# Pooling the next batch's keys on GpSimd: 256-column pieces, one per step, in place of a whole block every twelfth step

## The chip, the cores and the metric

The kernel runs on one core of a Trainium2 chip. The metric is the device time of one execution in microseconds; the time of a kernel is the median of its runs. The engines are named as in the profile: PE (TensorE) multiplies matrices, DVE (VectorE) and ACT (ScalarE) work elementwise, POOL (GpSimd) works elementwise too and issues indirect DMAs, SP (SyncE) issues the other DMAs.

## The reference

Attention with keys that are pooled 4 by 4 and projected, followed by a mixture of eight experts with one expert per row and a test that lets rows skip it:

```python
def _attn_ref(q, kv, w_sr):          # q (4, 12288, 128), kv (4, 384, 32, 128)
    kv_pool = kv.reshape(B, H // r, r, W // r, r, C).mean(axis=(2, 4))   # r = 4
    kv_flat = kv_pool.reshape(B, -1, C) @ w_sr                           # 768 keys a batch
    k = v = kv_flat
    s = scale * (q @ k.transpose(0, 2, 1))
    s = s - s.max(-1, keepdims=True)
    a = np.exp(s)
    a /= a.sum(-1, keepdims=True) + 1e-09
    return (a @ v).astype(np.float32)

def _moe_ref(x, w_skip, w_gate, w1, w2):   # x: the rows of the attention
    do_compute = x @ w_skip > 0
    out = x.copy()
    xc = x[do_compute]
    logits = xc @ w_gate
    e_idx = np.argmax(logits, axis=1)
    ...
    for e in range(E):
        mask = e_idx == e
        h = np.maximum(xc[mask] @ w1[e], 0.0)
        y[mask] = gate_w[mask, None] * (h @ w2[e])
    out[do_compute] = xc + y
    return out
```

## The kernel before

The program has two phases. The first is attention, one unrolled loop over 384 steps; a step is a tile of 128 query rows, and 96 steps are a batch. The second is a loop over groups of 2,048 rows for one expert each. The change lies in the first phase.

In step `t` the program records, in this order, `scores(t)` (six matmuls, L578 to L580), `attend(t - 6)` (18 matmuls with the probabilities as weights, L641), `p_transpose(t - 1)` (L616), the row maximum on DVE (L586), the exponential on ACT (L591), and for the tile before the split of the probabilities into two f16 halves: the high half on ACT (L595), the low half on DVE (L599, which reads `p_sb` and `p16`, both in SBUF). SP then transposes four of the six blocks by DMA (L603); the other two are transposed on PE and split by L623 (ACT) and L624 (DVE). DVE also inverts the row sums (L649, L651), which `attend` waits for through its accumulator's buffer.

Each engine runs its instructions in the order of recording and waits only where it needs another's result, so POOL can run ahead of the steps or fall behind them.

POOL's queue in the loop holds four kinds of work. Every fourth step it computes `q_lo` (L567), after ACT's `q_hi` (L566); the scores use it some six steps later. Every twelve steps a dozen finished tiles are routed to experts by `route`: POOL does part of it (L692 to L708, L721 `oh_all`, L756 `nxt` to L760), in turns with DVE, and PE counts rows with `oh_all` (L748, L749). It then issues twelve indirect DMAs, the scatters (L184), two per step. And it pools the keys of the next batch.

For that pooling SP loads a block of keys in four parts (`load_kv`, L413; the list `KV_T` of L897 sets the steps), at steps 9, 22, 35, 48, 61 and 74 of a batch the last part of blocks 0 to 5. Four steps after the last part the block's generator `pool_kv` joins the list `pools`. It halves the 2,048 columns of a partition by adds: 1,024, 512, 256 and a last add of 128 columns into `pooled`. The loop pops a generator only in steps with `tb % 12 == 11` (L964; `PSL` is 11) and runs it to its end there, so all four adds stand together. From step 84 on, `prep_kv` transposes and projects the pooled keys. Batch 0 has no step to hide in: most of its blocks are pooled on DVE (`pool_kv_first`), one by `pool_kv` in the prologue (L865). Batch 3 has no next batch, so nothing is pooled in its steps; pad rows are written there in place of the key loads.

Of the kernel before, what the change touches and what calls it, by code (L numbers as in the profile page):

```python
# [15 lines left out]
ALU = mybir.AluOpType  # L16
# [4 lines left out]
RT = 12  # L21
# [3 lines left out]
def kernel(  # L25
# [11 lines left out]
    nc = tc.nc  # L37
    NR, C, RT, P = q.shape
# [7 lines left out]
    E, _, FF = w1.shape  # L46
# [22 lines left out]
    PSL = 11  # L69
# [94 lines left out]
    def alloc_h(pool):  # L164
        h.update(hi=pool.tile([P, FC, ST], F16, name="h_hi"), lo=pool.tile([P, FC, ST], F16, name="h_lo"))

    op = ctx.enter_context(tc.tile_pool(name="op", bufs=2))
# [199 lines left out]
    with ExitStack() as p1:  # L367
# [32 lines left out]
        def write_pads(e, i):  # L400
            dst = scr[e * CAP + i * P:e * CAP + (i + PK) * P, :].rearrange("(p k) c -> p k c", p=P)
            no_dep(nc.sync.dma_start(dst, pad).ins, "scr")
# [5 lines left out]
        def load_kv(b, k, rs=range(R)):  # L408
            if rs[0] == 0:
                KVT[b, k] = kvp.tile([P, R, R * C], F32, name="kvt")  # L410
            src = kv[b, k * HG * R:(k + 1) * HG * R].rearrange("(i r) (g w) c -> r i g (w c)", r=R, w=R)
            for r in rs:
                nc.sync.dma_start(KVT[b, k][:, r, :], src[r])  # L413

        def pooled_out(b, k):
            if k == 0:
                pooled[b] = kprep.tile([P, KC, C], F32, name="pooled")
            return KVT.pop((b, k)), pooled[b][:, k, :]
# [12 lines left out]
        def pool_kv(b, k):  # L431
            t, o = pooled_out(b, k)
            f = t.rearrange("p r x -> p (r x)")
            n = R * R * C
            while n > 2 * C:
                n //= 2
                nc.gpsimd.tensor_tensor(out=f[:, 0:n], in0=f[:, 0:n], in1=f[:, n:2 * n], op=ALU.add)
                yield
            nc.gpsimd.tensor_tensor(out=o, in0=f[:, 0:C], in1=f[:, C:2 * C], op=ALU.add)

        HK = NK // 2
# [95 lines left out]
        def prep_kv(b):  # L537
            for f in (kv_transpose, k_matmul):
                for h in range(2):
                    f(b, h * HC, (h + 1) * HC)  # L540
                    yield
            yield from prep_v(b)
# [6 lines left out]
        def load_q(g):  # L549
            r, o = divmod(g, RG)  # L550
            q_sb[g] = qp.tile([P, GW], F32, name="q_sb")
            nc.sync.dma_start(q_sb[g], q[r][:, o * GT:(o + 1) * GT, :].rearrange("c t p -> c (t p)"))
# [5 lines left out]
        def run_late(q):  # L558
            while q:
                q.pop(0)()  # L560
# [9 lines left out]
        def scores(t):  # L570
            g, j = divmod(t, GT)
            k_hi, k_lo = KV[t // TPB][0:2]
            q_hi, q_lo = (x[:, j * P:(j + 1) * P] for x in qT[g])
            s = ps_s.tile([P, 2, 512], F32, name="s_ps")
            S_PS[t] = s
            for h in range(2):
                sl = slice(h * HK, (h + 1) * HK)
                nc.tensor.matmul(s[:, h, :HK], q_hi, k_hi[:, sl], start=True, stop=False)  # L578
                nc.tensor.matmul(s[:, h, :HK], q_hi, k_lo[:, sl], start=False, stop=False)  # L579
                nc.tensor.matmul(s[:, h, :HK], q_lo, k_hi[:, sl], start=False, stop=True)  # L580
# [3 lines left out]
        def row_max(t):  # L584
            NM[t] = small.tile([P, 1], F32, name="nm")
            nc.vector.tensor_reduce(out=NM[t], in_=S_PS[t][:, :, :HK], axis=AX.XY, op=ALU.max, negate=True)  # L586

        def row_exp(t):
            g, j = divmod(t, GT)
            P_SB[t] = pp.tile([P, 2, HK], F32, name="p_sb")  # L590
            nc.scalar.activation(out=P_SB[t], in_=S_PS.pop(t)[:, :, :HK], func=AF.Exp, bias=NM.pop(t))  # L591

        def p_hi(t):
            P16[t] = hl.tile([P, 2, KD * P], F16, name="p16")
            nc.scalar.activation(out=P16[t][:, 0, :], in_=p_flat(t)[:, 0:KD * P], func=AF.Copy, scale=2.0 ** PEXP)  # L595

        def p_lo(t):
            p16 = P16.pop(t)
            nc.vector.scalar_tensor_tensor(out=p16[:, 1, :], in0=p_flat(t)[:, 0:KD * P], scalar=2.0 ** PEXP,  # L599
                                           in1=p16[:, 0, :], op0=ALU.mult, op1=ALU.subtract)  # L600
            P_SB.pop(t)
            PT[t] = ptp.tile([P, 2 * KD, P], F16, name="pt")
            nc.sync.dma_start_transpose(PT[t], p16.rearrange("p a x -> p (a x)"))  # L603
# [6 lines left out]
        def p_transpose(t):  # L610
            g, j = divmod(t, PP)
            if j == 0:
                PTP[g] = acc_ps()
            p = p_flat(t)
            for i in range(KP):
                nc.tensor.transpose(PTP[g][:, (j * KP + i) * P:(j * KP + i + 1) * P],  # L616
                                    p[:, (KD + i) * P:(KD + i + 1) * P], ident)
            if j < PP - 1:
                return
            ps = PTP[g][:, 0:PP * KP * P]  # L620
            hl_t = ptq.tile([P, 2, PP * KP * P], F16, name="ptq")
            PTQ[g] = hl_t.rearrange("p a (j k x) -> p a j k x", j=PP, x=P)
            next_a.append(lambda: nc.scalar.activation(out=hl_t[:, 0, :], in_=ps, func=AF.Copy, scale=2.0 ** PEXP))  # L623
            next_v.append(lambda: nc.vector.scalar_tensor_tensor(  # L624
                out=hl_t[:, 1, :], in0=ps, scalar=2.0 ** PEXP, in1=hl_t[:, 0, :], op0=ALU.mult, op1=ALU.subtract))
# [268 lines left out]
        pools = []  # L894
# [14 lines left out]
        while t < NTILE + LAG - 1 or jobs:  # L909
            t += 1  # L910
            b, tb = divmod(t, TPB)
            live = t < NTILE
            for now, nxt in ((split_a, next_a), (split_v, next_v), (late_a, next_l)):
                now.extend(nxt)
                nxt.clear()
            if live:
                scores(t)
            if 0 <= t - LAG < NTILE:
                attend(t - LAG)
            if 0 <= t - 1 < NTILE:  # L920
                p_transpose(t - 1)
            if live:
                row_max(t)
            run_late(early_a)
            run_late(split_a)
            if 0 <= t - 1 < NTILE:
                p_hi(t - 1)
            run_late(late_a)
            if live:
                row_exp(t)  # L930
            run_late(early_g)
            run_late(split_v)
            run_late(early_v)
            if 0 <= t - 1 < NTILE:
                p_lo(t - 1)
            if live:
                if t % GT == 0 and t // GT + RG < NGRP:
                    load_q(t // GT + RG)
                if b + 1 < B:
                    for k, r in KV_T.get(tb, ()):  # L940
                        load_kv(b + 1, k, [r])
                if b + 1 < B and tb == PREP_T:
                    preps.append(prep_kv(b + 1))
                if t in PAD_T:
                    write_pads(*PADS.pop(0))
            first_step(NTILE - t)
            if t == NTILE:
                p_s.close()
                p_kv.close()
                alloc_h(p1.enter_context(tc.tile_pool(name="hp1", bufs=1)))  # L950
                ps_up = p1.enter_context(tc.tile_pool(name="ps_up", bufs=4, space=PSUM))
                alloc["h"] = lambda: ps_up.tile([P, ST], F32, name="up_ps")
            ph = t % GT
            if ph == 1 and t // GT + 2 < NGRP:
                q_split(t // GT + 2)
            ranked = run_jobs(ph)
            if preps and not ranked and (ph in (0, 3) or tb < LAG):
                if next(preps[0], "end") == "end":
                    preps.pop(0)
            if live and b + 1 < B:  # L960
                for k, r in KV_T.get(tb - 4, ()):
                    if r == R - 1:
                        pools.append(pool_kv(b + 1, k))
                if pools and tb % RT == PSL:  # L964
                    for _ in pools.pop(0):
                        pass
            for _ in range(2 * (t >= NTILE)):
                next(first)
        for _ in make_table():
# [76 lines left out]
```

## Time and profile before

| | us |
|---|---|
| median of 3 runs | 2067.53 |
| lowest, highest | 2058.41, 2076.75 |
| the profiled execution | 2057.81 |
| its span | 2056.1 |
| the attention loop's 384 steps, from the span's start | 35 to 1180 |
| mean granted TensorE clock | 0.949 |

The profiled execution is one run, 9.7 us under the median. Below, rows of the page and of the trace's views are shown as they stand. A row of instructions gives line, engine, operation, tiles, shapes and count, then busy time and mean duration in ns, then the engine's idle time just before them and what ended it. A row of waits gives who waited for what, the total in us, how often, and the longest. A row of a stage gives its limits and length, the busy time of each engine that is asked for with the count of instructions, and the granted clock, the DMA engines' busy share and GB/s. Batch 0 is steps 0 to 95, and so on; "dozen" stands for twelve steps from a multiple of twelve on.

### The profile page before, as it was taken

How to read it: one execution, taken by the hardware profiler on the slowest of the kernel's cores; microseconds unless marked ns; L12 is line 12 of the kernel's file. 1: busy time of each engine (PE TensorE's matmuls, PEld its weight loads, DVE VectorE, ACT ScalarE, POOL GpSimd, SP SyncE). 2: the span in 40 equal slices, each digit the busy share in tenths (PEclk: the TensorE clock that was granted, in tenths of full speed). 3: DMA queues.
4: the chain of work that ended last, by engine and by line, in shares of the span. 5: the costliest groups of instructions: out<-in, count | busy, mean ns of one | idle time of the engine just before them, and what ended most of it. 6: DMA issues, size and time to landing. Idle time of an engine off the chain costs nothing. (4 is left out here: it accounts for less than half of the span.)

```text
span 2056.1 us, 42524 instructions
## 1 busy us (share of the span) xinstructions
PE 1830.2 (89%) x13955; PEld 1308.1 (64%) x13955; DVE 1549.2 (75%) x3222; ACT 1302.8 (63%) x2480; POOL 1068.9 (52%) x1296
## 2 busy tenths in 40 slices
PE   4998888989898888898988867999999999999997
PEld 3987878878787787887878733444444444444443
DVE  7987857878686787776867746777777777777776
ACT  3876767767676676766767724656565655555564
POOL 2277674677756768655565753343333333333433
PEclk9999988999999899988999978999999999999999
DMA  7998988889789789878997832433333343333333
GB/s 173 209 193 173 184 165 165 182 157 167 147 161 170 156 177 184 169 164 175 191 185 169 176 73 74 107 98 88 92 88 92 88 103 100 94 90 90 91 89 88
DMA packets 620914, 284.61 MB, mean 138 GB/s; under 512 B 502112, under 2 KB 570848, under 8 KB 620768
## 3 DMA queue, kind: packets, MB, share of 16 engines
q1 hardware_dynamic: 599264, 244.30, 58.3%
q0 software_dynamic: 21504, 38.43, 6.2%
q8 instruction: 83, 1.36, 0.3%
q14 instruction: 63, 0.52, 0.1%
HBM read 90.60 MB, written 78.64 MB: 82 GB/s over the span
## 5 line engine op out<-in xcount | busy, mean ns | idle before, releaser
L184 POOL DMA_INDIRECT out_dram<-o,xin x288 | 299.7, 1040 | 510.7 <-DVE o L293 422.9
L586 DVE TENSOR_REDUCE nm<-s_ps 128x1 f32<-128x768 f32 x384 | 363.7, 947 | 208.7 <-PE s_ps L580 129.8
L270 DVE SCALAR_TENSOR_TENSOR h_lo<-h_ps,h_hi 128x512 f16<-128x512 f32 x544 | 343.1, 685 | 174.1 <-ACT h_hi L269 174.1
L591 ACT ACTIVATE p_sb<-s_ps,nm 128x768 f32<-128x768 f32 x384 | 346.5, 902 | 195.2 <-DVE nm L586 152.9
L184 POOL DMA_INDIRECT scr<-rows,di x384 | 385.5, 1004 | 149.6 <-issue 122.9
L641 PE MATMUL acc_ps<-v_hi,pt 128*128 128x138 f16 x3072 | 339.9, 232 | 90.8 <-DVE ptq L624 36.1
L641 PEld LDWEIGHTS <-pt 128*128 128x128 f16 x4608 | 294.2, 101 | 166.1 <-issue 164.9
L269 ACT ACTIVATE h_hi<-h_ps 128x512 f16<-128x512 f32 x544 | 298.9, 594 | 41.8 <-PE h_ps L268 17.9
L599 DVE SCALAR_TENSOR_TENSOR p<-p_sb,p 128x512 f16<-128x512 f32 x384 | 316.2, 824 | 1.6 <-ACT p L595 1.0
L578 PE MATMUL s_ps<-k_hi,q_hi 128*128 128x384 f32 x768 | 305.1, 397 | 7.6 <-issue 7.6
L641 PE MATMUL acc_ps<-v_lo,pt 128*128 128x138 f16 x1536 | 309.7, 231 | 2.2 <-issue 2.2
L579 PE MATMUL s_ps<-k_lo,q_hi 128*128 128x384 f32 x768 | 268.7, 350 | 4.9 <-issue 4.9
L580 PE MATMUL s_ps<-k_hi,q_lo 128*128 128x384 f32 x768 | 267.6, 348 | 5.7 <-issue 5.7
L595 ACT ACTIVATE p<-p_sb 128x512 f16<-128x512 f32 x384 | 242.0, 630 | 5.5 <-DMA pt<-p 2.2
L266 PE MATMUL h_ps<-xT,w_hi 128*128 128x512 f16 x544 | 206.1, 379 | 24.9 <-issue 24.9
L285 ACT ACTIVATE yT<-y_ps,y_sc 128x512 f32<-128x512 f32 x68 | 46.7, 687 | 276.9 <-PE y_ps L282 217.1
L282 PE MATMUL y_ps<-h_hi,w_hi 128*128 128x512 f16 x544 | 206.2, 379 | 0.0
L282 PE MATMUL y_ps<-h_hi,w_lo 128*128 128x512 f16 x544 | 206.2, 379 | 0.0
L268 PE MATMUL h_ps<-xT,w_lo 128*128 128x512 f16 x544 | 206.1, 379 | 0.0
L267 PE MATMUL h_ps<-xT,w_hi 128*128 128x512 f16 x544 | 206.1, 379 | 0.0
L282 PEld LDWEIGHTS <-w_hi 128*128 128x128 f16 x1152 | 113.4, 98 | 134.7 <-issue 4.5
L567 POOL TENSOR_TENSOR q_lo<-q_sb,q_hi 128x512 fp32r<-128x512 f32 x96 | 125.9, 1312 | 138.0 <-ACT q_hi L566 137.7
(215 smaller groups left out, 3283.7 us busy)
## 6 DMA issues: line engine op xcount, KB each, us to landing
kvt<-in_kv_dram SPq DMA_DIRECT2D x96, 256.0 KB
q_sb<-in_q_dram SPq DMA_DIRECT2D x96, 256.0 KB
out_dram<-rows SPq DMA_DIRECT2D x96, 256.0 KB
xin<-scr SPq DMA_DIRECT2D x75, 264.0 KB, 2.7
w_raw<-in_moe_w_dram SPq DMA_DIRECT2D x38, 512.0 KB, 4.0
scr<-pad SPq DMA_DIRECT2D x32, 264.0 KB
pt<-p SPq DMA_TRANSPOSE x384
scr<-rows,di POOLq DMA_INDIRECT x384
```

The costliest lines, as they stand in the source:

```text
L184: ins = nc.gpsimd.indirect_dma_start(out=dst, out_offset=bass.IndirectOffsetOnAxis(ap=ids, axis=0), in_=src, in_offset=None, bounds_check= ...
L269: nc.scalar.activation(out=h["hi"][:, c, :], in_=ps, func=AF.Relu)
L270: nc.vector.scalar_tensor_tensor(out=h["lo"][:, c, :], in0=ps, scalar=0.0, in1=h["hi"][:, c, :], op0=ALU.max, op1=ALU.subtract)
L282: nc.tensor.matmul(ps, w[:, c, :], h[x][:, c, :], start=(i == 0), stop=(i == len(terms) - 1))
L578: nc.tensor.matmul(s[:, h, :HK], q_hi, k_hi[:, sl], start=True, stop=False)
L579: nc.tensor.matmul(s[:, h, :HK], q_hi, k_lo[:, sl], start=False, stop=False)
L580: nc.tensor.matmul(s[:, h, :HK], q_lo, k_hi[:, sl], start=False, stop=True)
L586: nc.vector.tensor_reduce(out=NM[t], in_=S_PS[t][:, :, :HK], axis=AX.XY, op=ALU.max, negate=True)
L591: nc.scalar.activation(out=P_SB[t], in_=S_PS.pop(t)[:, :, :HK], func=AF.Exp, bias=NM.pop(t))
L595: nc.scalar.activation(out=P16[t][:, 0, :], in_=p_flat(t)[:, 0:KD * P], func=AF.Copy, scale=2.0 ** PEXP)
L599: nc.vector.scalar_tensor_tensor(out=p16[:, 1, :], in0=p_flat(t)[:, 0:KD * P], scalar=2.0 ** PEXP, in1=p16[:, 0, :], op0=ALU.mult, op1=ALU ...
L641: nc.tensor.matmul(ps[:, j % 2, :], w, v[a][:, k, :], start=(i == 0), stop=(i == len(AVL) - 1))
```

## The change

Each add of 1,024 or 512 columns is cut into adds of 256 columns, four and two of them, so that a block takes seven adds of 256 and the last one of 128. The generator yields after each of the seven. The loop no longer waits for the twelfth step: in every step it advances the first generator of the list once, from step 74 of a batch on twice. So block 0 is pooled in steps 13 to 20, block 1 in 26 to 33, block 2 in 39 to 46, block 3 in 52 to 59, block 4 in 65 to 72, and block 5 in 78 to 81. The sums are the same, in the same grouping. `pool_kv` in the prologue is cut in the same way.

```diff
@@ -432,10 +432,12 @@
             t, o = pooled_out(b, k)
             f = t.rearrange("p r x -> p (r x)")
             n = R * R * C
+            m = 2 * C
             while n > 2 * C:
                 n //= 2
-                nc.gpsimd.tensor_tensor(out=f[:, 0:n], in0=f[:, 0:n], in1=f[:, n:2 * n], op=ALU.add)
-                yield
+                for c in range(0, n, m):
+                    nc.gpsimd.tensor_tensor(out=f[:, c:c + m], in0=f[:, c:c + m], in1=f[:, n + c:n + c + m], op=ALU.add)
+                    yield
             nc.gpsimd.tensor_tensor(out=o, in0=f[:, 0:C], in1=f[:, C:2 * C], op=ALU.add)
 
@@ -961,9 +963,9 @@
                 for k, r in KV_T.get(tb - 4, ()):
                     if r == R - 1:
                         pools.append(pool_kv(b + 1, k))
-                if pools and tb % RT == PSL:
-                    for _ in pools.pop(0):
-                        pass
+                for _ in range(2 if tb >= 74 else 1):
+                    if pools and next(pools[0], "end") == "end":
+                        pools.pop(0)
```

The lines behind the first piece move by two in the kernel after (L437 becomes L439, L439 becomes L441, L567 becomes L569, and so on).

POOL's queue before, in the dozen of steps 24 to 35 of batch 0 (`scr<-rows,di` are the scatters, `oh_all` the table that PE's count waits for):

```order
L184 DMA scr<-rows,di 409600x132 x6
L567 TENSOR_TENSOR q_lo<-q_sb,q_hi 128x512
L184 DMA scr<-rows,di 409600x132 x2
L721 TENSOR_TENSOR oh_all_94<-oh,act 128x12x8
L184 DMA scr<-rows,di 409600x132 x2
L437 TENSOR_TENSOR kvt<-kvt 128x1024
L437 TENSOR_TENSOR kvt<-kvt 128x512
L437 TENSOR_TENSOR kvt<-kvt 128x256
L439 TENSOR_TENSOR pooled<-kvt 128x128
```

The same place after:

```order
L439 TENSOR_TENSOR kvt<-kvt 128x256
L184 DMA scr<-rows,di 409600x132 x2
L439 TENSOR_TENSOR kvt<-kvt 128x256
L184 DMA scr<-rows,di 409600x132 x2
L439 TENSOR_TENSOR kvt<-kvt 128x256
L184 DMA scr<-rows,di 409600x132 x2
L441 TENSOR_TENSOR pooled<-kvt 128x128
L569 TENSOR_TENSOR q_lo<-q_sb,q_hi 128x512
L184 DMA scr<-rows,di 409600x132 x2
L723 TENSOR_TENSOR oh_all_94<-oh,act 128x12x8
L184 DMA scr<-rows,di 409600x132 x2
```

The pooling has moved from behind the last scatters of the dozen to between the earlier ones, and ahead of `oh_all`.

POOL's queue before, in the last dozen of batch 0 but one, steps 78 to 83:

```order
L184 DMA scr<-rows,di 409600x132 x6
L567 TENSOR_TENSOR q_lo<-q_sb,q_hi 128x512
L184 DMA scr<-rows,di 409600x132 x2
L721 TENSOR_TENSOR oh_all_95<-oh,act 128x12x8
L184 DMA scr<-rows,di 409600x132 x2
L437 TENSOR_TENSOR kvt<-kvt 128x1024
L437 TENSOR_TENSOR kvt<-kvt 128x512
L437 TENSOR_TENSOR kvt<-kvt 128x256
L439 TENSOR_TENSOR pooled<-kvt 128x128
L449 MEMSET v_hi 128x6
```

The same place after, with two pieces in a step (the `v_hi` memset belongs to step 84):

```order
L439 TENSOR_TENSOR kvt<-kvt 128x256 x2
L184 DMA scr<-rows,di 409600x132 x2
L439 TENSOR_TENSOR kvt<-kvt 128x256 x2
L184 DMA scr<-rows,di 409600x132 x2
L439 TENSOR_TENSOR kvt<-kvt 128x256 x2
L184 DMA scr<-rows,di 409600x132 x2
L439 TENSOR_TENSOR kvt<-kvt 128x256
L441 TENSOR_TENSOR pooled<-kvt 128x128
L569 TENSOR_TENSOR q_lo<-q_sb,q_hi 128x512
L184 DMA scr<-rows,di 409600x132 x2
L723 TENSOR_TENSOR oh_all_95<-oh,act 128x12x8
L184 DMA scr<-rows,di 409600x132 x2
```

Here all eight adds come ahead of `q_lo` and `oh_all`. The queues of PE, DVE, ACT and SP hold the same work in the same order as before.

## The prediction

> **What bounds the kernel now.** The page comes first: which engine is busy where.
>
> ```profile
> PE 1830.2 (89%) x13955; PEld 1308.1 (64%) x13955; DVE 1549.2 (75%) x3222; ACT 1302.8 (63%) x2480; POOL 1068.9 (52%) x1296
> L586 DVE TENSOR_REDUCE nm<-s_ps 128x1 f32<-128x768 f32 x384 | 363.7, 947 | 208.7 <-PE s_ps L580 129.8
> L599 DVE SCALAR_TENSOR_TENSOR p<-p_sb,p 128x512 f16<-128x512 f32 x384 | 316.2, 824 | 1.6 <-ACT p L595 1.0
> ```
>
> The change touches only the attention loop, 384 steps (L586 runs once in each). An average hides that a dozen steps have two parts, so I asked for the stages of one dozen, all engines and then L586 alone, and for DVE's waits in each of them.
>
> ```profile
> 391.80:411.40 19.60, 19.60 (x220) 18.31 (x218) 19.08 (x39) 17.64 (x34) 10.83 (x19) 1.00 0.98 202
> 411.40:426.40 15.00, 10.88 (x93) 9.59 (x92) 7.27 (x15) 7.54 (x13) 12.88 (x13) 0.89 0.72 120
> 391.80:411.40 19.60, 8.46 (x9) 1.00 0.98 202
> 411.40:426.40 15.00, 2.87 (x3) 0.89 0.72 120
> DVE nm L586 <- PE s_ps L580: 0.3, 1, 0.3
> DVE nm L586 <- PE s_ps L580: 6.4, 2, 5.6
> ```
>
> (Rows 1 and 2: length, then PE, PEld, DVE, ACT, POOL busy, granted clock, DMA share, GB/s. Rows 5 and 6 belong to the first and the second stage.) Nine steps run smoothly in 19.60 us: PE is never idle, the DMA share is 0.98, and DVE is busy for 19.08 and waits for 0.3. The next three steps take 15.00 us: the clock falls to 0.89, DVE is half idle and waits for the scores. So in the smooth part DVE has 19.60 - 19.08 = 0.52 us to spare per dozen, and in the stalled part it has 7.73.
>
> The pooling of before runs at the seam. Here it is in the timeline of that dozen:
>
> ```profile
> 386.41 4.90 POOL L437 TENSOR_TENSOR kvt<-kvt 128x1024 f32<-128x1024 f32 x3
> 386.89 2.47 DVE L599 SCALAR_TENSOR_TENSOR p<-p_sb,p 128x512 f16<-128x512 f32 x1
> 390.98 0.28 PE L641 MATMUL acc_ps<-v_hi,pt 128*128 128x138 f16 x2 [0.18 <-DVE rs L649]
> 395.69 0.69 DVE L599 SCALAR_TENSOR_TENSOR p<-p_sb,p 128x512 f16<-128x512 f32 x1
> ```
>
> L599, which takes 0.69 us undisturbed, takes 2.47 when it meets a pooling add; PE loses 0.18 us by it here. The Trainium skill, "SBUF — State Buffer", section "Who interferes with whom", says that a VectorE instruction with two SBUF inputs (L599 is one) contends with a GpSimd instruction that reads SBUF, and that the second one to issue blocks until the first has finished. These rows agree.
>
> **The change part by part.** What the adds cost on POOL now, by shape:
>
> ```profile
> L437 POOL TENSOR_TENSOR kvt<-kvt 128x1024 f32<-128x1024 f32 x19 | 45.4, 2389 | 15.1 <-DMA kvt<-in_kv_dram 14.9
> L437 POOL TENSOR_TENSOR kvt<-kvt 128x512 f32<-128x512 f32 x19 | 28.9, 1519 | 1.5
> L437 POOL TENSOR_TENSOR kvt<-kvt 128x256 f32<-128x256 f32 x19 | 17.8, 936 | 1.5
> L439 POOL TENSOR_TENSOR pooled<-kvt 128x128 f32<-128x128 f32 x19 | 10.7, 561 | 1.5
> L437 POOL TENSOR_TENSOR kvt<-kvt x57: 722/1602/2419, 19.8 to 859.2; 128x1024 f32<-128x1024 f32 x19, 128x512 f32<-128x512 f32 x19, 128x256 f32<-128x256 f32 x19
> ```
>
> *POOL time.* A block was 2.39 + 1.52 + 0.94 + 0.56 = 5.4 us; it becomes seven pieces of 0.72 (the fastest seen) to 0.94 (the mean) and the last add, 5.6 to 7.1 us. Over 18 blocks in the loop that is 4 to 31 us more. POOL has room for it:
>
> ```profile
> POOL nxt L756 <- DVE pre L752: 127.4, 28, 6.8
> POOL q_lo L567 <- ACT q_hi L566: 109.2, 43, 9.2
> ```
>
> It idles 127.4 us before `nxt` and 109.2 before `q_lo` in the loop, so this costs nothing by itself.
>
> *What is taken away: the long blocks of L599.* Three stages of 72 steps each, the first two with five blocks pooled (L437 alone, 15 adds), the third with none; then L599 alone; then the two waits of PE that DVE ends, stage by stage:
>
> ```profile
> 349.80:561.10 211.30, 24.86 (x15) 0.93 0.86 165
> 636.70:852.40 215.70, 24.33 (x15) 0.94 0.88 175
> 932.00:1148.40 216.40, 0.00 (x0) 0.93 0.89 183
> 349.80:561.10 211.30, 60.15 (x72) 0.93 0.86 165
> 636.70:852.40 215.70, 64.09 (x72) 0.94 0.88 175
> 932.00:1148.40 216.40, 53.53 (x73) 0.93 0.89 183
> PE acc_ps L641 <- DVE ptq L624: 9.4, 4, 2.7
> PE acc_ps L641 <- DVE rs L649: 4.3, 6, 3.4
> PE acc_ps L641 <- DVE ptq L624: 9.7, 3, 4.1
> PE acc_ps L641 <- DVE rs L649: 8.9, 7, 3.7
> PE acc_ps L641 <- DVE ptq L624: 6.5, 4, 2.7
> PE acc_ps L641 <- DVE rs L649: 5.2, 3, 2.5
> ```
>
> On DVE: 72 undisturbed-by-pooling L599 cost 53.53 x 72/73 = 52.8, so pooling added 7.4 and 11.3 us, 18.7 over ten blocks, 1.87 a block, 33.6 us over 18. That is the gain if every blocked microsecond were on the path. On PE: its waits for DVE are 13.7 and 18.6 us with pooling, 11.7 without: 2.0 + 6.9 over ten blocks, 0.89 each, 16 us over 18. On the clock of the wall: 72 steps take 211.30 and 215.70 us with pooling and 216.40 without, so pooling costs nothing that can be seen (the third stage has the pad writes in place of the key loads, near enough the same DMA share). Bounds 0 and 33.6; I take 8, between the wall's 0 and PE's 16, since the block falls where PE is cold and DVE has been idle.
>
> *What is put in: 126 pieces, most of them in the smooth part,* where DVE has 0.52 us a dozen. How often does a short POOL add catch L599? From the stage without pooling: L599 takes 53.53/73 = 0.733 there against 0.69 undisturbed, 0.043 x 73 = 3.2 us, and this row of L567 alone gives the adds of `q_lo` that mostly did it:
>
> ```profile
> 932.00:1148.40 216.40, 23.34 (x18) 0.93 0.89 183
> ```
>
> 3.2/23.34 = 0.135 us of block per us of such an add. The pieces and last adds are 18 x 5.6 = 101 us of POOL, so 13.6 us; a piece is 0.72/1.30 as long, so the mean block is shorter: 7.5. From the other side, by L437 itself: 33.6 us of block for 18 x 5.4 = 97 us, 0.35 per us; the block grows with the add's length, and the length that a us of adding sits in falls from (2.39² + 1.52² + 0.94²)/4.85 = 1.84 to about 0.8, so 101 x 0.35 x 0.8/1.84 = 15 us. Of 7.5 to 15 us, the spare 0.52 x 18 = 9 takes some: 0 to 15 on the path; I take 6, nearer the `q_lo` row, which was measured in that very part.
>
> *Moves with one answer.* The pieces stand ahead of `oh_all` now, up to six of them, 6 x 0.72 = 4.3 us; the matmul that waits for it comes 10.7 us after it:
>
> ```profile
> 194.32 0.64 POOL L721 TENSOR_TENSOR oh_all<-oh,act 128x96 bf16<-128x96 f32 x1
> 205.69 0.21 PE L748 MATMUL misc<-oh_all,ones_bf 128*128 128x104 bf16 x1
> ```
>
> So 6 us remain, and it costs nothing; without the stall in between it would cost PE a few us in that dozen. The first piece asks for a load issued four steps before (some 9 us); of the DMAs whose landing the page gives, the nearest in size took
>
> ```profile
> xin<-scr SPq DMA_DIRECT2D x75, 264.0 KB, 2.7
> ```
>
> so POOL should seldom wait, and what would be queued behind it (`q_lo`, the scatters) is wanted later still. In the prologue one block also runs in pieces, 0.2 to 1.7 us later; PE waits there for POOL now, but afterwards for DVE for longer:
>
> ```profile
> 24.87 0.47 PE L454 MATMUL acc_ps<-ident,pooled 128*128 128x128 f32 x1 [1.61 <-POOL pooled L439]
> 31.58 0.47 PE L454 MATMUL acc_ps<-ident,pooled 128*128 128x128 f32 x1 [3.43 <-DVE pooled L428]
> ```
>
> 3.43 us of slack covers it. For prep at step 84 the pooled keys are ready earlier than before; nothing waited there.
>
> *Sum.* -8 + 6 = -2 us. The profiled execution took 2057.8 us (span 2056.1), so 2056; the median of the runs is 2067.5, 9.7 above it, so I forecast 2065 as a median.
>
> **The rivals.**
>
> A. *Every block was on the path (faster).* The end of the smooth part is late by what L599 loses at the seam, and the pieces vanish in gaps. For it: PE's waits for `rs` and `ptq` are longer with pooling. Against it: the wall shows nothing. Gain 33.6 less 0 to 7.5: about 30 us, 2037.
>
> B. *DVE becomes the bound in the smooth part (slower).* POOL, freed by the same event each time (`q_hi` from ACT, `pre` from DVE), starts its pieces at the same point of a step, and that point lies in L599. Place: the nine smooth steps of the 18 dozens. If each of 126 pieces catches one L599 at half its length, 0.36 us, that is 45 us; less 9 of spare and the 8 gained, +28: 2095. It decides from about 0.52 + 0.44 us of new block per dozen on, that is when a piece costs more than 0.14 us. Against it: `q_lo`, equally freed by ACT, costs 3.2/18 = 0.18 us at 1.30 us of length, so 0.1 for a piece. The same section of the skill's SBUF page speaks for B: of two such instructions it tells to schedule whichever is off the critical path, and the pieces go to where DVE has least room.
>
> C. *The stall itself moves.* The 15.00 us of the three stalled steps are 15 - 3 x 2.18 = 8.5 us over the smooth pace. It comes in the stage without pooling too (216.40 us for 72 steps), so pooling isn't its cause; but pieces between the scatters change the traffic ahead of it. Were one in five of 18 stalls to go or to double, 3.6 x 8.5 = 31 us either way; I put it into A's and B's chances.
>
> D. *It does not do what it says:* where POOL isn't held by a wait, pieces of several steps run back to back, since POOL takes them as its queue comes. They still free DVE between two, so this changes little; it lies in the forecast.
>
> **How the numbers follow.** About 1% (20 us) is what a measurement of this kernel tells from no change. No change: 0.57 (2065, own range 2048 to 2083: a gain of 33.6 with a cost of 15 is 19 under 2067.5, a cost of 15 with no gain 15 over it). Faster, A with its part of C: 0.24, about 2037. Slower, B with its part of C: 0.19, about 2095. The range reaches from 2038 to 2092, which leaves out about half of A and of B.
>
> **What would show it.** Right: L599's longest rows fall from 2.47 to under 1.5 us, its sum in the 72-step stages from 60 and 64 to about 56; PE's waits for `rs` and `ptq` fall to the third stage's 11.7; the smooth nine steps stay at 19.6 to 20. Wrong on the cost side: smooth stretches of 21 us and more with DVE busy throughout and PE waiting for it. Wrong on the gain side: 72-step stages under 205 us. Wrong on C: stalls of another length, or in other steps.

## The result, and the profile after

| | before | after |
|---|---|---|
| median, us | 2067.42 (4 runs) | 1996.34 (4 runs) |
| lowest, highest | 2058.41, 2076.75 | 1988.27, 2000.38 |
| ratio, with its 95% interval | | 0.9651 [0.9598, 0.9704] |
| the profiled execution: time, span | 2057.81, 2056.1 | 1995.29, 1992.7 |

The kernel after is 3.5% faster. The forecast was 2065 us with a range down to 2038, so it was wrong.

The page of the kernel after has these rows for the engines, for the row maximum and for the instruction that the forecast expected to be blocked less:

```profile
PE 1802.1 (90%) x13955; PEld 1284.9 (64%) x13955; DVE 1560.5 (78%) x3222; ACT 1300.6 (65%) x2480; POOL 1095.2 (55%) x1372
L588 DVE TENSOR_REDUCE nm<-s_ps 128x1 f32<-128x768 f32 x384 | 363.7, 947 | 138.5 <-PE s_ps L582 73.9
L601 DVE SCALAR_TENSOR_TENSOR p<-p_sb,p 128x512 f16<-128x512 f32 x384 | 315.9, 823 | 1.8 <-ACT p L597 0.6
```

L601 (L599 before) takes what it took: 315.9 us in place of 316.2. What fell is the time that DVE waits for the scores ahead of the row maximum: 129.8 to 73.9 us. So the gain isn't where the change was expected to act.

The stages of 72 steps (steps 12 to 83 of batches 1 and 2, which have pieces, and of batch 3, which has none) in the kernel after; first all engines, then L601 alone:

```profile
331.40:514.60 183.20, 174.28 (x1874) 159.73 (x1874) 171.84 (x312) 149.60 (x274) 150.93 (x203) 1.00 0.99 189
595.50:783.10 187.60, 175.75 (x1875) 160.72 (x1875) 170.25 (x312) 149.99 (x274) 151.10 (x204) 0.99 1.01 198
869.50:1082.30 212.80, 187.82 (x1890) 171.01 (x1888) 162.56 (x333) 151.51 (x276) 121.62 (x167) 0.94 0.90 185
331.40:514.60 183.20, 64.42 (x72) 1.00 0.99 189
595.50:783.10 187.60, 63.70 (x72) 0.99 1.01 198
```

Before, these stages took 211.30, 215.70 and 216.40 us. The two with pieces are 28.1 us shorter each, the one without by 3.6 only. L601 sums to 64.42 and 63.70 there (60.15 and 64.09 before), so it is blocked for no less time in all. Sorted over the whole run by what POOL did meanwhile, that is made of two shifts: the rows of L601 that overlap a pooling add exceed the undisturbed 0.69 us by 18.9 us in sum (26.1 before), and those that overlap a `q_lo` add alone by 29.4 us (22.0 before).

One dozen (steps 24 to 35 of batch 1) shows where the 28 us come from. Its first ten steps and its last two, in the kernel before and then in the kernel after:

```profile
386.02:410.32 24.30, 24.12 (x246) 22.23 (x246) 23.75 (x43) 20.00 (x36) 15.55 (x22) 0.94 0.88 178
410.32:421.77 11.45, 7.33 (x70) 6.36 (x68) 4.53 (x10) 5.34 (x11) 9.47 (x10) 0.91 0.67 116
```

```profile
361.86:386.11 24.25, 22.10 (x237) 20.07 (x237) 23.52 (x44) 19.80 (x36) 20.48 (x29) 1.00 0.97 193
386.11:391.58 5.47, 5.47 (x67) 5.16 (x65) 5.40 (x11) 5.13 (x11) 4.66 (x6) 1.00 1.10 196
```

The first ten steps are as long as before. The last two took 11.45 us and take 5.47: the stall of step 10 is gone. Of the 18 dozens with pieces, 17 had a step of 5 us or more among their last three before (the first of them, steps 12 to 23 of batch 0, has no scatters yet and had none); after, none has. From the first row maximum of each dozen to the next, those 18 dozens sum to 633.5 us before and 554.0 after, 79.5 us less, while the three dozens from step 84 and the three from step 0 took 9.0 and 7.7 us more; with the rest the loop is 63.8 us shorter, and the span 63.4.

What stands at that place in POOL's queue: the timeline of POOL, first of the kernel before, then of the kernel after (start, duration, instruction, and in brackets the idle time before it).

```profile
408.48 0.21 POOL L708 TENSOR_TENSOR na<-na,idt 128x12 f32<-128x12 f32 x1
409.21 1.07 POOL L184 DMA_INDIRECT scr<-rows,di  x1 [0.52 <-issue]
410.58 0.97 POOL L184 DMA_INDIRECT scr<-rows,di  x1 [0.30 <-issue]
...
415.67 0.97 POOL L184 DMA_INDIRECT scr<-rows,di  x1 [0.30 <-issue]
416.65 1.29 POOL L567 TENSOR_TENSOR q_lo<-q_sb,q_hi 128x512 fp32r<-128x512 f32 x1
```

```profile
385.44 1.08 POOL L184 DMA_INDIRECT scr<-rows,di  x1 [0.15 <-issue]
386.82 0.97 POOL L184 DMA_INDIRECT scr<-rows,di  x1 [0.30 <-issue]
387.80 0.76 POOL L439 TENSOR_TENSOR kvt<-kvt 128x256 f32<-128x256 f32 x1
388.72 0.99 POOL L184 DMA_INDIRECT scr<-rows,di  x1 [0.17 <-issue]
```

Before, six scatters run one behind the other, some 1.3 us apart (409.21 to 415.67); after, a piece stands behind every two. And this is PE in the kernel before while the six run:

```profile
415.06 0.27 PE L616 MATMUL acc_ps<-ident,p_sb 128*128 128x128 f32 x1 [1.03 <-issue]
416.48 0.43 PE L578 MATMUL s_ps<-k_hi,q_hi 128*128 128x384 f32 x1 [0.63 <-issue]
419.68 0.39 PE L641 MATMUL acc_ps<-v_hi,pt 128*128 128x138 f16 x2 [2.42 <-DVE ptq L624]
```

From 414.0 us on, 5 us after the first of the six, PE has gaps that "issue" stands for, that is, it waits for nothing that the profile shows; then it waits for DVE, which got its scores late. The granted clock is lower only after that, as two stretches of this dozen show (all engines, as above):

```profile
413.40:418.10 4.70, 2.16 (x14) 1.32 (x11) 0.13 (x1) 1.11 (x2) 3.91 (x4) 1.00 0.75 142
418.10:421.77 3.67, 2.09 (x19) 2.12 (x20) 2.43 (x5) 2.17 (x4) 3.34 (x4) 0.71 0.01 0
```

In the first PE is busy for less than half of the time, at a full clock; in the second the clock is 0.71. The Trainium skill, "TensorE: Matmul & The Clock Gate", section "What's actually happening", has the clock go to half after an idle window of about 3.4 us; the rows agree in kind. So in this dozen the lower clock follows the stall and does not start it.

The waits of PE over the whole span, "issue" in the loop's lines and the new one, before and then after:

```profile
PE acc_ps L641 <- issue: 25.2, 30, 4.2
PE s_ps L578 <- issue: 7.6, 14, 1.1
PE acc_ps L616 <- issue: 7.3, 12, 1.0
PE s_ps L580 <- issue: 5.7, 10, 1.0
PE s_ps L579 <- issue: 4.9, 8, 1.0
```

```profile
PE misc L750 <- POOL oh_all L723: 21.7, 12, 4.0
PE acc_ps L643 <- issue: 15.8, 21, 5.0
```

The five rows of before are 50.7 us; after, the loop's lines have 27.9 (15.8 and four rows of 2.3 to 4.1). Against that stands a wait that wasn't there: the count of PE waits for `oh_all`, 21.7 us, of which 4.0 in step 87 of each of the batches 0 to 2.

### The profile page after: what moved, and what is told of

It is laid out like the page before. It is cut to its first block, busy times and chain, and to the rows that moved or that the text cites. A ratio compares the mean times of both kernels' runs of the same rounds, so it can differ in the third digit from the quotient of the medians.

```text
span 1992.7 us, 42614 instructions
## 1 busy us (share of the span) xinstructions
PE 1802.1 (90%) x13955; PEld 1284.9 (64%) x13955; DVE 1560.5 (78%) x3222; ACT 1300.6 (65%) x2480; POOL 1095.2 (55%) x1372
## 5 line engine op out<-in xcount | busy, mean ns | idle before, releaser
L588 DVE TENSOR_REDUCE nm<-s_ps 128x1 f32<-128x768 f32 x384 | 363.7, 947 | 138.5 <-PE s_ps L582 73.9
L184 POOL DMA_INDIRECT scr<-rows,di x384 | 393.3, 1024 | 137.5 <-issue 108.1
L643 PE MATMUL acc_ps<-v_hi,pt 128*128 128x138 f16 x3072 | 331.5, 228 | 48.9 <-DVE rs L651 23.1
L643 PEld LDWEIGHTS <-pt 128*128 128x128 f16 x4608 | 286.3, 100 | 121.6 <-issue 120.3
L601 DVE SCALAR_TENSOR_TENSOR p<-p_sb,p 128x512 f16<-128x512 f32 x384 | 315.9, 823 | 1.8 <-ACT p L597 0.6
L643 PE MATMUL acc_ps<-v_lo,pt 128*128 128x138 f16 x1536 | 302.6, 227 | 1.0 <-issue 1.0
L580 PE MATMUL s_ps<-k_hi,q_hi 128*128 128x384 f32 x768 | 300.3, 391 | 2.3 <-issue 2.3
L266 PE MATMUL h_ps<-xT,w_hi 128*128 128x512 f16 x544 | 206.6, 380 | 26.1 <-issue 26.1
L282 PE MATMUL y_ps<-h_lo,w_hi 128*128 128x512 f16 x544 | 195.1, 379 | 0.0
```

What stands on the lines that cost most here:

```text
L184: ins = nc.gpsimd.indirect_dma_start(out=dst, out_offset=bass.IndirectOffsetOnAxis(ap=ids, axis=0), in_=src, in_offset=None, bounds_check= ...
L282: nc.tensor.matmul(ps, w[:, c, :], h[x][:, c, :], start=(i == 0), stop=(i == len(terms) - 1))
L643: nc.tensor.matmul(ps[:, j % 2, :], w, v[a][:, k, :], start=(i == 0), stop=(i == len(AVL) - 1))
```

## The experiments

Four theories were tested. S: scatters that stand in a row on POOL stall PE, and the pieces break the rows up. D: what was gained are the long blocks of L599. P: the pieces slow the smooth steps a little, PE is no longer without a gap, and the stall is the price of a stretch without one. C: the stall belongs to the chip of the first runs; where it doesn't come, the pieces only cost. Q came up later: where there is no stall, POOL sets the length of a dozen.

A call is a set of runs made together on one chip. The kernel before ran in every call, and it took 1897 us in some of them and 2058 to 2081 in others. Ratios are to the kernel before of the same call.

**e1, e2: cut alone, place alone.** e1 is the kernel after with all pieces of a block in step 11. e2 is the kernel before with this hunk the other way round: its uncut adds are issued one per step, two from step 74 of a batch on.

```diff
-                for _ in range(2 if tb >= 74 else 1):
-                    if pools and next(pools[0], "end") == "end":
-                        pools.pop(0)
+                if pools and tb % RT == PSL:
+                    for _ in pools.pop(0):
+                        pass
```

> The kernel before with the adds cut into 256 columns, but all eight run together in the twelfth step as before. Theory S (the stall in step 10 of a dozen comes when POOL issues four or more scatters one behind the other, and the pieces take it away because they stand between the scatters): the queue around the scatters is as before, so the stall stays, 7 to 8 us for that step in all dozens, and the time is 2050 to 2075. Theory D (what was gained is the long block of the DVE instruction L599, which the cut takes away): 2035 or less, and with the whole gain 1996. Theory P (the pieces slow DVE in the smooth part, PE is no longer busy without a gap, and so its clock is not lowered): as S, 2050 to 2075.

> The kernel before with the adds uncut (1024, 512, 256, 128 columns) but one per step, two from step 74 on. Adds then stand between scatters in the dozens of blocks 3, 4 and 5 of a batch, and ahead of them in those of blocks 0 and 1. Theory S: the stall in step 10 goes in the dozens where an add parts the scatters (about half of the 18), so 2010 to 2040, and it stays in those of blocks 0 and 1. Theory D: L599 is blocked for as long as before, and now in the smooth part, so 2067 or more. Theory P: an add of 2.4 us slows DVE more than a piece does, so the stall goes in every dozen with an add in steps 1 to 9, blocks 0 and 1 included, 1990 to 2020.

Measured: 1907.64 us, 1.0060 [1.0044, 1.0077], and 1908.86 us, 1.0076 [1.0059, 1.0093]. The kernel before took 1896.70 us there. In neither is a step with index 9 to 11 of a dozen 5 us long or more, although e1's scatters stand in rows of six: in this call there was nothing to remove, and the two edits are told apart by nothing but their small costs.

**e3, e4: something between the scatters, and fewer of them in a step,** both made from the kernel before.

```diff
                 if j % 2 == 0 and j > 0 and r < LASTR - 1:
+                    nc.gpsimd.memset(gap, 0.0)
                     yield
```

```diff
-                if j % 2 == 0 and j > 0 and r < LASTR - 1:
+                if j > 0 and (r < SNAPR or (j % 2 == 0 and r < LASTR - 1)):
                     yield
```

> The kernel before, pooling untouched, with a memset of 768 columns on POOL (about 0.7 us, it reads nothing from SBUF) behind each pair of scatters. Theory S: the stall goes in every dozen, those of batch 3 too; 31 dozens at 5 us, less what a late oh_all costs PE (0 to 4 us a dozen): 1910 to 2000. Theory D: L437 blocks L599 as before, so 2060 to 2075. Theory P: DVE isn't slowed, since a memset doesn't read SBUF, so the stall stays: 2060 to 2080.

> The kernel before with one scatter per step in place of two, up to the route that the first expert's load waits for. Nothing else. Theory S: POOL is no longer behind, at most two or three scatters stand together, and the stall goes in most of the 27 dozens: 1930 to 1990. Theories D and P: nothing that they name is touched, 2055 to 2075.

Measured: 1982.65 us, 1.0464 [1.0446, 1.0481], and 1902.71 us, 1.0031 [1.0019, 1.0044]. Again no stall to remove. The 150 memsets are 114.8 us of POOL and cost 86 us of time, so POOL has little room here. What of it is POOL's length isn't told apart, since the sum of L599 rose too, from 343.5 us (e8, the kernel before) to 377.5.

**e5: the kernel after itself.**

> The changed kernel once more, beside the kernel before. In the four runs before this one the kernel before took 1897 us where it had taken 2067, and two kernels close to the change did not gain. Theory S (the scatters standing together cause the stall by themselves): 0.965 of the kernel before wherever it runs. Theory C (the stall is a state of the chip on which the first runs were made: there PE crawls for some 5 us a dozen; the pieces avoid it there, and where there is no stall they only cost): on a chip where the kernel before takes 1897, between 1.00 and 1.01 of it, 1897 to 1916; on one where it takes 2067, 0.965.

Measured: 1894.49 us against 1897.78, 0.9985 [0.9975, 0.9994]. The dozens with pieces take 553.0 us in all, as they did in the first runs (554.0). So what differs between the two calls in these dozens is not the kernel after, but the kernel before. That the change gains next to nothing where there is no stall is as theory C has it (it said 1.00 to 1.01); that it is the chip that decides is not shown, as the end of the next section says.

**e6: the last block of a batch back at the seam,** to give step 87 its `oh_all` in time.

```diff
-                for _ in range(2 if tb >= 74 else 1):
+                for _ in range(1 if tb < 74 else 8 if tb % RT == PSL else 0):
```

> The kernel after, but the pieces of each batch's last block (from step 74 on) stand together behind the last scatters of step 83, as before the change, so that oh_all is computed ahead of them. In the kernel after PE's count in step 87 of batches 0 to 2 waited 4.2 us each time for oh_all, and those three steps took 7.4 to 7.7 us in place of 2.4. If the late oh_all is the reason, these three steps take 2.3 to 3 us here and the kernel is 10 to 15 us under the kernel after: 0.990 to 0.994 of before where before takes 1897 us. If the count waits for something else as well (the scan's operands, q_lo), the steps stay above 5 us and the ratio at 0.998. Where before takes 2067 us, theory S (scatters that stand together stall PE) adds that the stall of step 10 is back in the dozen from step 72, some 5 us in each of three batches, which cancels the gain: 1990 to 2000 us.

Measured: 1888.33 us, 0.9951 [0.9934, 0.9969]. Step 87 fell to 2.6 us as expected (6.8 to 7.7 in e5), but step 88 rose to 7.9 to 8.2 us (4.3 to 5.0 in e5): there PE transposes the pooled keys, and now it waits for the block (8.5 us in three waits). Half of the expected gain turned into a new wait.

**e7: DVE slowed instead of POOL moved.**

```diff
+            if t >= 18 and live and 1 <= tb % RT <= 9:
+                nc.vector.tensor_reduce(out=gap, in_=ones_f, axis=AX.X, op=ALU.max)
```

> The kernel before, with one small extra reduction of 128 columns on DVE in each step with index 1 to 9 of a dozen, from step 18 on; its result is not used. It takes DVE's spare time in the smooth steps and leaves POOL as it was. Theory P (the pieces slow the smooth steps a little, PE is no longer without a gap there, and so no stall follows): where before takes 2067 us, the stall of step 10 goes and the kernel comes to 1990 to 2030 us. Theory S: the stall stays and the kernel takes 2070 to 2100 us. Where before takes 1897 us there is no stall to remove, and both expect it slower: some 9 x 0.2 us in each of 30 dozens, less what gaps take, 1.005 to 1.03 of before.

Measured: 1919.18 us, 1.0121 [1.0102, 1.0140], with no stall to remove. It says nothing on P.

**e8: the kernel before in such a call.**

> The kernel before without an edit, for its rows on the chip of these runs. Theory C (the stall belongs to the chip of the first runs): if the time is near 1897 us, step 10 of a dozen takes 2.3 to 3 us and no dozen is above 31 us; if it is near 2067 us, step 10 takes 7 to 8 us. Theory S: step 10 takes 7 to 8 us at either time.

Measured: 1897.77 us, one run. Step 10 takes 1.9 to 2.3 us in all dozens but the loop's last, as C expected; its other sign, no dozen above 31 us, missed, since most dozens with pooling take 31.6 to 33.3. A dozen with pooling and one of batch 3, and what POOL waits for in such a dozen:

```profile
344.62:376.24 31.62, 29.07 (x317) 26.71 (x314) 29.06 (x54) 24.92 (x47) 26.62 (x33) 1.00 1.02 195
915.72:945.10 29.38, 28.87 (x317) 26.69 (x314) 27.00 (x54) 24.98 (x47) 20.99 (x29) 1.00 1.14 213
POOL scr L184 <- issue: 3.7, 11, 0.6
POOL scr L184 <- POOL rows L772: 1.0, 1, 1.0
```

(The last two rows are from 376.24 to 408.06.) Without the stall a dozen with pooling is 2.2 us longer than one without, and POOL in it waits for no other engine: it is busy, or between two scatters.

**e9: the halving adds left out** of the blocks pooled in the loop.

```diff
-                nc.gpsimd.tensor_tensor(out=f[:, 0:n], in0=f[:, 0:n], in1=f[:, n:2 * n], op=ALU.add)
+                if b == 0:
+                    nc.gpsimd.tensor_tensor(out=f[:, 0:n], in0=f[:, 0:n], in1=f[:, n:2 * n], op=ALU.add)
```

> The kernel before without the adds of 1,024, 512 and 256 columns of the blocks pooled in the loop (the prologue's block keeps them); only the last add of 128 columns is left, so the keys of batches 1 to 3 are sums of 2 of the 16 values in place of 16. It leaves 18 x 4.85 us of POOL's work out. Theory Q (where step 10 doesn't stall, POOL is the engine that sets the length of a dozen with pooling: 26.6 us busy and 3.4 us between scatters of 31.8): a dozen that took 31.7 us comes to the 29.5 us of the dozens of batch 3, so some 13 full dozens x 2.2 us = 29 us less, with the three of step 84 up to 40: 0.979 to 0.986 of before where before takes 1897 us. Rival N (POOL's length is beside the point, the block costs only what L599 and the waits for rs lose, 13 us in the change): 0.993 or more. Where before takes 2067 us, theory S expects the stalls to stay, since the scatters still stand together: 2045 to 2067 us.

Measured: 2050.43 us against 2060.18, 0.9945 [0.9912, 0.9978]. This call met the stall. With nothing left of the long adds PE still has it:

```profile
PE acc_ps L642 <- issue: 24.2, 31, 4.3
PE acc_ps L617 <- issue: 9.4, 15, 1.3
PE s_ps L579 <- issue: 7.8, 16, 1.1
```

Theory D fell: without any long add the sum of L599 is 25.6 us lower than in the kernel before of the first runs (290.6 in place of 316.2), and yet the time falls by 10 us and not by 71; and the stall has no need of pooling.

**e10: adds between all scatters.** The kernel after with an add on an unused tile where no piece is waiting.

```diff
+            if live and t >= 18 and tb % RT >= 6 and (b + 1 == B or dry):
+                nc.gpsimd.tensor_tensor(out=gap[:, 0:256], in0=gap[:, 0:256], in1=gap[:, 256:512], op=ALU.add)
```

> The kernel after, with an extra add of 256 columns on POOL (on a tile that is not used) in the steps with index 6 to 11 of each dozen in which no piece is waiting: batch 3 and the ends of the batches get something between their scatters too. Theory S: where before takes 2067 us, the stalls that the kernel after keeps (steps 84 to 95 and 0 to 11 of a batch, and batch 3) go, some 14 dozens x 5 us: 1900 to 1940 us. Theory P (a stall follows a stretch in which PE had no gap): they stay, 1990 us or more. Where before takes 1897 us there is nothing to gain; by theory Q POOL has 5 us of slack in those dozens, against 6 x 0.75 us: 0.998 to 1.006 of before.

Measured in the same call: 1959.04 us, 0.9497 [0.9448, 0.9545].

```profile
PE misc L752 <- POOL oh_all L725: 42.6, 23, 4.0
PE acc_ps L645 <- issue: 1.4, 5, 0.4
```

"Issue" is 1.4 us in place of the 15.8 that the kernel after had on that line in the first runs, and the stall is gone from all but two of the dozens that kept it in the kernel after: work that nobody needs made the kernel faster. It is 19 us slower than theory S expected, since POOL now brings `oh_all` late 23 times.

**e11, e12: e4 and e1 again,** where there is a stall.

> The kernel before with one scatter per step in place of two (up to the batch's last steps; pooling stands at the seam as before). It adds no work to POOL and puts other work, or a wait, between the scatters: no six of them stand together any more. Theory S (six scatters in a row stall PE): where before takes 2060 us the stalls of step 10 go, and with them some 30 x 5 us: 1900 to 1940 us, a ratio of 0.92 to 0.945. Rival W (it is the adds on POOL that keep PE running, not the room between the scatters): the stalls stay, 2040 us or more. Where before takes 1897 us: 1.003, as in the run of this edit there.

> The kernel after with the adds cut to 256 columns, but all pieces of a block together in step 11, where the blocks stood before. Theory S: the scatters stand six in a row as before, so where before takes 2060 us the stalls stay, and the cut gives nothing: 2050 to 2085 us. If the cut itself (short adds) and not the place gave the gain: 1990 to 2000 us. Where before takes 1897 us: 1.006, as in the run of this edit there.

Measured: 1952.02 us, 0.9477 [0.9431, 0.9522], and 2060.71 us, 1.0015 [0.9983, 1.0048]. PE's waits, one fence for each:

```profile
PE acc_ps L641 <- DVE rs L649: 58.8, 68, 2.5
PE acc_ps L641 <- issue: 8.2, 7, 4.3
```

```profile
PE acc_ps L643 <- issue: 18.5, 27, 4.2
PE s_ps L581 <- issue: 7.8, 17, 1.0
```

These two decide. e12 has all of the cut and none of the move and gains nothing; e11 leaves the pooling as it was before the change, adds no work, only takes the scatters apart, and gains more than the change did. It is 12 us slower than S expected; its waits for `rs` are those of e4, 59.7 us, so they come with the edit. Two things stay untested where there is a stall: the move without the cut (e2 ran only without one), and whether it is the row that counts or the rate, since what parts the scatters also makes them fewer in a given time. P falls as well, by two stages of the kernel before in the first runs, up to its first row of six scatters (they start from 115.06 to 121.91 us):

```profile
63.00:92.00 29.00, 29.00 (x325) 27.07 (x324) 25.99 (x47) 25.59 (x49) 8.68 (x12) 1.00 1.04 224
92.00:120.00 28.00, 28.00 (x308) 26.06 (x306) 25.87 (x50) 24.40 (x45) 16.47 (x23) 1.00 1.07 191
```

PE is busy in all of these 57 us at a clock of 1.00, with no stall; the first one comes at 122 us, under that row.

**e13 to e15: longer rows, e9 once more, and both edits together.** e13 has four scatters in a step; e15 is the kernel after with e4's edit.

```diff
-                if j % 2 == 0 and j > 0 and r < LASTR - 1:
+                if j % 4 == 0 and j > 0 and r < LASTR - 1:
```

> The kernel before with four scatters per step in place of two: POOL's queue holds rows of eight scatters where it held rows of six. Theory S, with the stall's size going by the row's length: where before takes 2060 us, step 10 (or the step where the eight stand) stalls by 5 x 8/6 = 7 us in place of 5, 30 x 2 = 60 us more: 2090 to 2140 us. If a stall has one size once it occurs: 2050 to 2080 us. Where before takes 1897 us: with eight in a row the stall may come there too, 1900 + 30 x 3 = 1990 us or more, against 1890 to 1915 us if the length of the row isn't what decides there.

> The kernel before without the adds of 1,024, 512 and 256 columns of the blocks pooled in the loop, as in e9; 18 x 4.85 us of POOL's work are left out. Where before takes 2060 us: 0.9945 as in e9. Where before takes 1897 us, theory Q (POOL sets the length of a dozen with pooling): 1857 to 1870 us, 0.979 to 0.986. Rival N (it does not): 0.993 or more.

> The kernel after with one scatter per step in place of two. Theory S: both edits remove the same stalls, so where before takes 2060 us the gains don't add; what remains is the stall in no dozen and the waits for oh_all: 1915 to 1955 us, 0.93 to 0.95. If they were two gains of their own, 0.965 x 0.948 = 0.915: 1885 us. Where before takes 1897 us: 0.9985 and 1.003 together, 0.998 to 1.004.

Measured: 2124.84 us, 1.0227 [1.0196, 1.0257]; 2067.32 us, 0.9929 [0.9903, 0.9956]; 1944.29 us, 0.9357 [0.9327, 0.9388]. The kernel before took 2080.87 us. In e13 the waits of the first line alone are:

```profile
PE acc_ps L641 <- issue: 77.3, 119, 2.6
```

A dozen of e13 has a row of four scatters in steps 7 and 8 and a row of eight in steps 9 to 11. By the median of the full dozens step 8 takes 4.1 us, where it takes 2.0 in the kernel before with a row of two: four scatters in a row stall PE too. Under the row of eight the steps 9 to 11 take 15.7 us together, and in e14, of the same call and with rows of six, 14.8; their means are 14.5 and 14.7. So eight are not shown to cost more than six. The 44 us that e13 lost are no more than the new stalls under its rows of four come to, some 27 x 2.1 us, and S's range was met by another way than S had it. In e15 the gains don't add (0.965 x 0.948 would be 0.915). Its 0.9357 is the lowest ratio where there is a stall; it wasn't run where there is none.

**e16: e9 where there is no stall.**

> The kernel before without the adds of 1,024, 512 and 256 columns of the blocks pooled in the loop, as in e9 and e14; 18 x 4.85 us of POOL's work are left out. Where before takes some 2065 us: 0.993 to 0.995 as there. Where before takes 1897 us, theory Q (POOL sets the length of a dozen with pooling): 1857 to 1870 us, 0.979 to 0.986. Rival N (it does not): 0.993 or more.

Measured: 1863.80 us against 1898.34, 0.9812 [0.9795, 0.9829]. The dozen that took 31.62 us in e8:

```profile
334.20:364.00 29.80, 29.10 (x317) 26.74 (x315) 27.41 (x54) 24.96 (x47) 21.37 (x30) 1.00 1.07 205
```

POOL loses 5.25 us of work, the dozen 1.8 us, and then PE is busy in 29.10 of 29.80. Q's number came out, with a limit: leaving the adds out also frees L599, and its sum falls from 343.5 to 315.5 us, so what of the 34.5 us is POOL's length and what is that block isn't told apart.

Counted in POOL's rows of the loop, and in the steps with index 9 to 11, without the loop's last dozen:

| | rows of 6 or more scatters | dozens with a step of 5 us or more there |
|---|---|---|
| before; after (first runs) | 29; 12 | 28; 10 |
| e9, e12, e14 | 29, 29, 29 | 27, 26, 28 |
| e13 (rows of 8) | 29 | 26 |
| e10, e11, e15 | 0, 2, 2 | 2, 1, 1 |
| e8, e1, e16 (before takes 1897 us) | 29, 29, 29 | 0, 0, 0 |

## Why the prediction was wrong

- *What bounds the kernel:* right in its rows. The dozen had a smooth part and a stall of some 8.5 us, and the stall was written down as the place where PE is cold and DVE idle. It was taken as given, though, and all terms of the sum were looked for beside it. POOL's room was read the same way: the 127.4 us before `nxt` and 109.2 before `q_lo` are 41.0 and 42.6 in e8's loop, where there is no stall.
- *The gain from the long blocks of L599* (8 of 0 to 33.6): not there where the forecast was made. The sum over the stages stayed, 64.42 and 63.70 us against a forecast of about 56; L601's longest row is 2.16 us (3.39 before) against a forecast of under 1.5. PE's waits for `rs` and `ptq` fell to 4.5 and 6.5 us there, but with the stall, which had made `ptq` late. In a call without a stall PE's wait for `rs` did fall, 34.5 to 19.3 us (e8, e5).
- *The cost of the pieces* (6 of 0 to 15): near in size. The pieces block L601 for 18.9 us against the forecast 7.5 to 15, and `q_lo`, which now runs at other places, for 7.4 more than before; together they took what the blocks gave back.
- *`oh_all` costs nothing:* wrong, 21.7 us of waits. The slack of 10.7 us was read in a dozen whose stall had made it; the text said that without the stall PE would lose a few us there, and it lost 4.0 in each of three dozens. Those are the ones behind block 5, where all eight adds stand ahead of `oh_all`, and not the six that the sum went by:

```profile
258.74 0.25 PE L750 MATMUL misc<-oh_all,ones_bf 128*128 128x104 bf16 x1 [4.04 <-POOL oh_all L723]
```

- *Rival C, the stall itself moves:* this is the step that failed. Its reasoning that the stall comes without pooling too was right (e9, e14: pooling is not its cause). Its sign was open and its size set at one stall in five, by no row. All 17 went, and the prediction's own sign for that, 72-step stages under 205 us, came with 183.20 and 187.60. The price of one, 8.5 us, was too high: 78.6/17 = 4.6 us. In part that is because it was taken over a pace of 2.18 us a step, and without the stall the dozen shown needs 29.72/12 = 2.48; that the smooth steps kept their pace only by what the stall gave back to POOL and DVE is likely, but not shown. Had the six scatters in a row been looked at beside PE's "issue" rows, both in the trace of before, the rival could have had a mechanism, and with it a chance of its own.
- *Rivals A, B, D:* A named the direction, but not what moved: with no long add left at all the kernel before gains 10 and 14 us where there is a stall (e9, e14), not the 71 of the change. B's sign did not come (the advice that it cites stands in the Trainium skill, "SBUF — State Buffer", under "Summary: rules for kernel authors"). D was seen: two pieces run back to back where POOL had been held.
- *No change as the likeliest case* is what the same kernel does where the kernel before has no stall: 0.9985. That is luck: there a gain in PE's waits for `rs` (15.2 us) and `p_sb` (16.5 to 3.1) is paid for by `oh_all` (1.3 to 28.3), 28.6 against 27.0 us, where the sum had 8 against 6, and `oh_all` at nothing.

Not settled: what in PE is held up while scatters run in a row, and why only in some calls. No view names it, since "issue" is the lack of a releaser. Late data are unlikely, since L579 waits too and reads the `q_hi` that L578 has just read. A late load of PE's instructions doesn't fit every stall: around the gaps that start at 1032.9 us in the kernel before, the nearest packets of the instruction queues in the trace are at 1025.4 and 1042.7 us. The stall was met in four of eight calls, counting the first runs; one chip number (0) came up with it and without it, so whether it goes with the chip isn't known. Nor is it all that differs: of the 161 us between the spans of the kernel before in the first runs and in e8, 19 lie behind the loop, and the loop of e11 is still 29.5 us longer than that of e4, the same kernel, with no step of 5 us or more left among those counted above but one.

## What to carry to other kernels

When the profile shows a stall that ends on "issue", look at what every other queue issues in the 5 us ahead of it, and give "the stall goes" a chance and a price of its own before summing small terms. Where such a stall is met, keep rows of indirect DMAs on POOL short: spread them over steps, or put work that is needed anyway between them. Where it isn't met this gains nothing: spreading cost 0.3% (e4) and filling with idle work 4.6% (e3). A slack that is read beside a stall may be a part of the stall, and go when the stall goes.

## What the runs showed of the hardware

- In four of eight calls six indirect DMAs of 128 rows one behind the other on POOL, some 1.3 us apart, held PE up for some 5 us (step 10 takes 7.6 us by the median of the full dozens, and 2.3 in e8). PE's first "issue" gap of 0.25 us or more starts 4.6 to 5.5 us after the first of them in 21 of the 29 rows of six of the kernel before. Four in a row cost 2.1 us (e13). The same instruction streams show nothing of it in the other calls.
- One kernel took 1897 us in some calls and 2058 to 2081 in others, some 9% apart, and an edit that is worth 5% where it is slow (e11: 0.9477) costs 0.3% where it is fast (e4: 1.0031).
